# A scan fused with a gated feed-forward layer: decay rows loaded once, one chunk of them four times, and the opening reordered

## The chip, the cores and the metric

The kernel runs on one core of a Trainium2 chip. The metric is the device time of one execution in microseconds; a version's time is the median over its runs.

## What is computed

Two blocks follow each other. The first is a chunked state-space scan over 4 batches, 8 heads and 768 positions, with head width 32 and state width 16:

```python
log_a = np.log(np.clip(a, 1e-06, 1.0))
for c in range(nc):                       # chunks of 32 positions
    cum = np.cumsum(la, axis=-1)          # la, xc, Bc, Cc: this chunk
    L = np.exp(cum[:, :, :, None] - cum[:, :, None, :]) * causal
    M = np.einsum('bhin,bhjn->bhij', Cc, Bc) * L
    y_intra = np.einsum('bhij,bhjd->bhid', M, xc)
    y_inter = np.einsum('bhin,bhnd->bhid', Cc, state) * np.exp(cum)[:, :, :, None]
    y[:, :, sl] = y_intra + y_inter
    state = decay_full * state + np.sum(Bx, axis=2)
```

Its output, seen as 3072 tokens of 256 values, goes through the second block: `h = x @ w_in`, `g = h * sigmoid(1.702 h)`, `g @ w_out`, with 2048 hidden columns. The two weight matrices come in 64-bit floating point; the kernel turns them into 32-bit itself.

## The kernel before, in words

**Tiling.** The 768 positions are six groups (g) of 128, each of 4 batches, so 512 tokens. A group has two pairs (p) of batches; a pair's scan is worked out in sub-chunks of 64 positions (two SIDES). The hidden layer has 16 blocks (f) of 128 columns. Group 0 uses plain matmuls: `hidden(0, f)` for the 16 blocks, then `project_all(0)`. The later groups use a scheme with seven products of sums and differences. The order on each engine is the order of the program: `in_order` at the end of the kernel ties each instruction to the one before it on its engine, so an instruction that waits holds everything behind it on that engine.

**The weights.** They come in ten pieces (`PIECES`): pieces 0 to 3 hold two blocks of w_in each, 4 and 5 four blocks each, 6 to 9 four blocks of w_out each. `fetch(i)` issues two DMAs for a piece on SyncE's queue (SP), into one of four buffers; with `held=True` a small memset on VectorE (DVE) comes first, so that the DMA can't start ahead of that place in VectorE's order. A 64-bit number becomes a 32-bit one in steps: `fields(i)` on VectorE (step 0 takes the exponent bits, L188; step 1 the mantissa bits, L191), `clamp(i)` with two activations on ScalarE (ACT, L200 and L202), `rounded(i)` (L206) and `join(i)` (L220, L226) on VectorE. `narrow(i)` is `rounded(i)`, then `fields(i + 1)`, then `join(i)`: VectorE takes the next piece's fields before it joins the current piece, so a next piece that is not there yet holds the join too. `join` also fetches the pieces after the sixth (`NEXT`).

**The opening, group 0.** `az0` holds the first 128 positions of `a`, replicated four times over the partitions. From it come the sums of logarithms (`cum`); TensorE (PE) builds their differences (`differ`), ScalarE takes the exponentials (L529): one of 1024 columns for pair 0, four of 384 for pair 1. GpSimd (POOL) copies each pair's last decays into `drops` (`drop_of`, L452) and makes `CsT` (L583). VectorE turns blocks of C and B (`turn_blocks`, L541). Then `score` (L597) makes the scores of both pairs, `turn_back` (L555) transposes B back into positions, `weigh` (L608) multiplies the decays by the scores, in halves, `ends_first` (L458) multiplies the turned B by `drops`, `finish` (L724, L709) makes the outputs of the scan, `gain` (L628) the increment of the state, and `keep_first` (L644, ScalarE) copies it into the state S. In `finish`, `dense` (L416) issues products of ones into an unused part of a PSUM bank: they fill TensorE's time and no one reads them. `pads` does so with small ones at the very start.

**The decay rows of the later groups.** The tile `az` holds all 768 positions of `a` for 32 rows (batch, head), replicated four times: 128 partitions of 3 KB. One DMA loads it behind `fetch(5)`. `clip` limits it on VectorE and sets the first element of each sub-chunk to 0. `pick_a` (L372) takes chunk 1 of it on ScalarE, the only chunk taken so, for the decays of pair 2, which `fan_all` spreads on TensorE (L395). `store_a` writes the clipped rows to a scratch in device memory (32 partitions), from which `spread` (L259) reads the decays of the other pairs back, broadcast over partitions. `clip` stands in `store_a`, that is behind hidden block 5.

**Around the change** the work of the opening is written out by hand in the order in which the diff shows it. Behind it, `in_hidden[0]` lists what follows each hidden block: block 4 the loads of C and B for group 1 (GpSimd's queue, held by VectorE), block 5 `store_a`, block 6 `pick_a`, blocks 2 to 9 `narrow(1)` and on.

Of the kernel before, what the change touches and what calls it, by code (L numbers as in the profile page):

```python
# [8 lines left out]
FP32 = mybir.dt.float32  # L9
U32 = mybir.dt.uint32  # L10
BF16 = mybir.dt.bfloat16
AF = mybir.ActivationFunctionType
# [4 lines left out]
P = 128  # L17
# [18 lines left out]
def kernel(  # L36
# [66 lines left out]
    dram = ctx.enter_context(tc.tile_pool(name="dram", bufs=1, space=bass.MemoryType.DRAM))  # L103


    az = ffn.tile([P, 4 * TG // 2], FP32, tag="mg", name="az", bufs=3)[:, :NC * P].rearrange(
        "p (c s) -> p c s", c=NC)
    az0 = const.tile([P, P], FP32, name="az0")
    cum = const.tile([P, 2, P], FP32, name="cum")
    w_in = const.tile([P, NF, NK, P], FP32, name="w_in")  # L110
# [5 lines left out]
    def place(p):  # L116

        c, n = divmod(p, PG)
        return c, 2 * n
# [38 lines left out]
    def fetch(i, queue=nc.sync, held=False):  # L158
        name, f, n = PIECES[i]
        if n == 2 and f % 4:  # L160
            t = pieces.pop(i - 1)[:, 2 * n * DM:]
        else:
            t = pieces[i] = words(f"bits{i}")
            t = t[:, :2 * n * DM]
        if held:
            nc.vector.memset(t[:, :1], 0)
        if name == "in":
            src = moe_w_in[:, 2 * f * P:2 * (f + n) * P].rearrange("(k p) e -> p k e", p=P)
            dst, src = (v.rearrange(s, h=n, e=2 * P) for v, s in (
                (t, "p (h k e) -> k p h e"), (src, "p k (h e) -> k p h e")))  # L170
        else:
            src = moe_w_out[f * P:(f + n) * P, :].rearrange("(f p) (h e) -> h p f e", p=P, h=2)
            dst = t.rearrange("p (h f e) -> h p f e", h=2, f=n)
        for k in range(2):
            queue.dma_start(out=dst[k], in_=src[k])
        t = t.rearrange("p (e w) -> p e w", w=2)
        bits[i] = t[:, :, 0], t[:, :, 1]
# [156 lines left out]
    def fold_ident(k, engine=nc.vector):  # L334

        engine.tensor_tensor(
            out=idents[:, k * NH:(k + 1) * NH],
            in0=ident[:, :H].unsqueeze(1).to_broadcast([P, NH, H]),
            in1=ident[:, H:].unsqueeze(1).to_broadcast([P, NH, H]), op=ALU.add)
# [18 lines left out]

    def clip(t):

        nc.vector.tensor_scalar(out=t, in0=t, scalar1=1e-6, scalar2=1.0,
                                op0=ALU.max, op1=ALU.min)
        nc.vector.memset(t.rearrange(by_chunk, s=2)[:, :, :, 0], 0.0)

    def pick_a(p):

        c, b = place(p)
        X = ffn.tile([P, 2, DM], FP32, tag="ob", name=f"X{p}")
        X = fans[p] = X.rearrange("p k (q i) -> p k q i", q=Q)
        for k in range(2):  # L370
            for q in range(Q):
                nc.scalar.activation(X[:, k, q], az[:, c], AF.Copy, scale=pick[:, b + k, q:q + 1])  # L372


    Ls, BE, st = {}, {}, {}
# [32 lines left out]
    def pads(n, t):  # L408

        for i in range(n):  # L410
            c = 32 * (i % R)
            nc.tensor.matmul(out=t[c:c + 32, :32], lhsT=ones[:32, :32], rhs=ones[:32, :32],
                             start=True, stop=True, tile_position=(0, c), skip_group_check=True)

    def dense(t, n=4, start=True):
        nc.tensor.matmul(out=t[:, :n * H], lhsT=ones,  # L416
                         rhs=ones[:, :H].unsqueeze(1).to_broadcast([P, n, H]),
                         start=start, stop=True, skip_group_check=True)
# [167 lines left out]
    def score(pairs):  # L586

        cb = area(f"cb{pairs[0]}").rearrange("p r (k e) -> p r k e", k=2 * PG)
        for n, p in enumerate(pairs):
            s = st[p]  # L590
            BT, CT = s["BT"], s.pop("CT")
            s["cb"] = cb[:, :, 2 * n:2 * n + 2]
            for k in range(2):
                for i, side in enumerate(SIDES):
                    for r in range(R):
                        rows = slice(32 * r, 32 * r + 32)
                        nc.tensor.matmul(  # L597
                            out=s["cb"][side, r, k].rearrange("p (q i) -> p q i", q=Q),
                            lhsT=BT[rows, k, side], rhs=CT[rows, k, :, side],
                            start=True, stop=True, tile_position=(32 * r, H * i),  # L600
                            skip_group_check=True)

    def weigh(p, ks=(slice(0, 2),)):

        Lv = Ls[p].rearrange("p k r q i -> p k r (q i)")
        cb = st[p]["cb"].rearrange("p r k e -> p k r e")
        for k in ks:
            nc.vector.tensor_tensor(out=Lv[:, k], in0=Lv[:, k], in1=cb[:, k], op=ALU.mult)  # L608
# [66 lines left out]
    def finish(pairs, steps=range(2)):  # L675
# [58 lines left out]
        if early:  # L734
            def copied(i, t):
                nc.scalar.activation(
                    yT[g][:, t, cols].rearrange("p (k s i) -> p s k i", s=2, i=H)[:, i], y[i][t],
                    AF.Copy)

            if 0 in steps:  # L740
                dense(begun_y["banks"][0][:, 2 * P:])
                intra(0, pairs[0])
                return
            dense(begun_y["banks"][0][:, 2 * P:])
            intra(1, pairs[1])
            for t in range(NK):
                copied(0, t)
            for t in range(NK):
                for n, p in enumerate(pairs):
                    inter(n, p, (t,))  # L750
                copied(1, t)
        else:
            for step in steps:
                for n, p in enumerate(pairs):
                    (inter, intra)[step](n, p)
            if 1 not in steps:
                return
            for i in range(2):
                nc.scalar.activation(  # L759
                    yT[g][:, :, cols].rearrange("p t (k s i) -> p s t k i", s=2, i=H)[:, i], y[2][:, i],  # L760
                    AF.Copy)
# [287 lines left out]
        differ(p, [(r, ab[p, r]) for r in range(R)])  # L1049

    busy = bank("busy")
    pads(30, busy)
    both = area("ab0")
    for r in range(R):
        mask_banks(0, r, both[:, r])
# [19 lines left out]
    firsts[0] = ssd.tile([P, NB, P], FP32, tag="first", name="first", bufs=1)  # L1075
    nc.gpsimd.memset(firsts[0], 0.0)
    turn_blocks(0, "B")
    score(range(PG))
    turn_back()
    fold_ident(1)  # L1080
    weigh(0, (slice(0, 1),))
    fetch(1, held=True)
    weigh(0, (slice(1, 2),))
    for p in range(PG):
        ends_first(p)
    for i in range(2, 6):
        fetch(i, held=i == 2)
    nc.sync.dma_start(out=az.rearrange("p c s -> p (c s)"), in_=a.rearrange(
        "b h s -> (b h) s").unsqueeze(0).to_broadcast([R, NB * NH, NC * P]))
    fields(0, (0,))  # L1090
    for k in range(2):
        weigh(1, (slice(k, k + 1),))
    fields(0, (1,))
    rounded(0)
    finish(range(PG), (0,))
    gain(range(PG), (0,))
    clamp(0)
    keep_first(0)
    finish(range(PG), (1,))
    join(0, 2, (0,))  # L1100
# [12 lines left out]
    in_hidden = [{} for _ in range(NG)]  # L1113
    in_project = [{} for _ in range(NG)]
    def store_a():
        clip(az)
        for i, side in enumerate(SIDES):
            nc.sync.dma_start(out=scratch[:, i].rearrange("c r i -> r c i"), in_=az[:32, :, side])

    at(in_hidden[0], 4, lambda: gain(range(PG), (1,)), lambda: keep_first(1))  # L1120
    at(in_hidden[0], 5, store_a)
# [221 lines left out]
```

## Time and profile before

| what | value |
|---|---|
| runs shown | 353.86, 351.01, 354.13 us; median 353.86 |
| profiled execution | 352.01 us, of which the span is 350.3 us |
| TensorE busy | 341.9 us (98%) |
| VectorE / ScalarE / GpSimd busy | 255.8 / 149.5 / 40.7 us |
| bytes moved by DMA | 26.02 MB |
| granted TensorE clock | 1.0 |

All times are from the profiled execution and count from the start of its span. In the rows of a timeline stand start, duration, engine, line, operation, written tile and read tiles, shapes and count; a bracket holds the idle time of the engine just before and what ended it. A row with a count over one merges neighbours. "SPq" is the issue of a DMA on SyncE's queue, with the time that the issue took, not the transfer. "issue" is time in which the engine waited for nothing that the profile shows. In a row of windows stand, for each stretch, its length, each engine's busy time and count, the granted clock, the mean busy share of the DMA engines and the GB/s that they moved.

### The profile page before, as it was taken

To read this page: it belongs to the slowest core of one execution; us is meant where nothing else is said; L and a number is where in the kernel's file an instruction comes from. 1 tells how busy PE (TensorE), PEld (TensorE's weight loads), DVE (VectorE), ACT (ScalarE), POOL (GpSimd) and SP (SyncE) were. 2 spreads that over 40 slices of the span, in tenths; PEclk is the share of its full clock that TensorE was granted. 3 is DMA by queue.
4 is the path that set the end of the run, shared out by engine and by line. 5 is a ranking of instruction groups with operands and counts; after the bars stand their busy time and mean duration, and the time that the engine had idled before them with its cause. 6 is when DMAs were issued, how large, how long until landed. Compare 5 with 4: busy or idle time off the path is not lost.

```text
span 350.3 us, 8534 instructions
## 1 busy us (share of the span) xinstructions
PE 341.9 (98%) x3514; PEld 281.1 (80%) x3514; DVE 255.8 (73%) x476; ACT 149.5 (43%) x333; POOL 40.7 (12%) x78
## 2 busy tenths in 40 slices
PE   8897999999999999999999999999999999999996
PEld 6666874545688888888888888888888888899996
DVE  7787999999789988749986557986454654455463
ACT  6767774005254322743442444433554321554320
POOL 8305500300297000000000000000000000000000
PEclk9999999999999999999999999999999999999999
DMA  5699986533529000466122326120000120000221
GB/s 136 187 296 253 279 180 148 87 72 59 94 57 189 2 0 5 74 129 100 23 35 60 52 78 120 21 33 9 0 4 2 17 33 12 1 2 0 33 31 60
DMA packets 82784, 26.02 MB, mean 74 GB/s; under 512 B 68841, under 2 KB 81001, under 8 KB 82745
## 3 DMA queue, kind: packets, MB, share of 16 engines
q1 hardware_dynamic: 79864, 23.41, 32.0%
q0 software_dynamic: 1888, 1.74, 2.2%
q8 instruction: 27, 0.44, 0.5%
q10 hardware_dynamic: 992, 0.33, 0.4%
q14 instruction: 13, 0.10, 0.1%
HBM read 22.22 MB, written 3.24 MB: 73 GB/s over the span
## 4 chain that ended last, share of the span: by engine, by line
PE 79%; DVE 8%; DMA 6%; POOL 3%; SPq 2%; issue 1%; ACT 1%; POOLq 0%; DVEq 0%
PE acc L944 28%; PE X L842 19%; PE Y L852 14%; PE acc L951 7%; DMA bits<-in_moe_w_out_dram 4%; PE y L724 3%; PE h L786 2%; PE y L709 2%; PE o L884 2%; DVE p L220 2%; SPq L269 1%; PE cb L597 1%; DMA a<-scratch 1%; DVE m L206 1%; DVE L L608 1%
## 5 line engine op out<-in xcount | busy, mean ns | idle before, releaser
L847 ACT ACTIVATE ac<-X 128x256 f32<-128x256 f32 x76 | 29.0, 382 | 80.0 <-PE X L842 79.6
L944 PE MATMUL acc<-mg,mw 128*128 128x256 f32 x192 | 54.5, 379 | 0.0
L971 DVE TENSOR_TENSOR gT<-Y,ac 128x512 f32<-128x512 f32 x38 | 26.2, 690 | 37.2 <-PE Y L852 33.9
L819 ACT ACTIVATE gT<-gT 128x512 f32<-128x512 f32 (+1 forms) x76 | 39.3, 519 | 31.7 <-DVE gT L971 31.1
L842 PE MATMUL X<-my,mi 128*128 128x256 f32 x152 | 45.1, 379 | 0.0
L971 DVE TENSOR_TENSOR gT<-Y,b 128x256 f32<-128x256 f32 x38 | 15.8, 418 | 34.0 <-PE Y L852 34.0
L944 PEld LDWEIGHTS acc<-mg,mw 128*128 128x128 f32 x192 | 36.5, 190 | 5.0
L786 PE MATMUL h<-yT,w_in 128*128 128x128 f32 (+2 forms) x182 | 36.3, 357 | 2.0 <-DVE w_in L226 1.8
L944 PE MATMUL acc<-gT,w_out 128*128 128x256 f32 x128 | 35.5, 379 | 0.0
L786 PEld LDWEIGHTS h<-yT,w_in 128*128 128x128 f32 x182 | 26.8, 191 | 10.3 <-issue 5.6
L842 PEld LDWEIGHTS X<-my,mi 128*128 128x128 f32 x152 | 28.0, 190 | 3.7
L884 PE MATMUL o<-gT,w_out 128*128 128x512 f32 x64 | 28.6, 597 | 0.0
L810 DVE TENSOR_TENSOR mg<-gT 128x512 f32<-128x512 f32 x40 | 27.2, 680 | 0.0
L944 PEld LDWEIGHTS acc<-gT,w_out 128*128 128x128 f32 x128 | 24.2, 190 | 3.4 <-ACT yT L759 0.2
L847 ACT ACTIVATE b<-X 128x256 f32<-128x256 f32 x38 | 14.6, 383 | 20.4 <-PE X L842 20.0
L842 PE MATMUL X<-yT,w_in 128*128 128x256 f32 x76 | 23.2, 389 | 0.0
L852 PE MATMUL Y<-yT,w_in 128*128 128x256 f32 x76 | 22.7, 381 | 0.0
L852 PE MATMUL Y<-my,mi 128*128 128x256 f32 x76 | 22.6, 379 | 0.0
L842 PE MATMUL X<-my,w_in 128*128 128x256 f32 x76 | 22.6, 381 | 0.0
L852 PE MATMUL Y<-yT,mi 128*128 128x256 f32 x76 | 22.5, 379 | 0.0
L884 PEld LDWEIGHTS o<-gT,w_out 128*128 128x128 f32 x64 | 11.8, 190 | 13.2 <-issue 12.7
L387 DVE TENSOR_TENSOR_SCAN L<-a,idents 128x1024 f32<-128x1024 f32 x9 | 20.5, 2274 | 0.0
(140 smaller groups left out, 569.3 us busy)
## 6 DMA issues: line engine op xcount, KB each, us to landing
a<-scratch SPq DMA_DIRECT2D x18, 256.0 KB
bits<-in_moe_w_out_dram SPq DMA_DIRECT2D x8, 512.0 KB
x<-in_x_dram SPq DMA_DIRECT2D x20, 128.0 KB
bits<-in_moe_w_in_dram SPq DMA_DIRECT2D x8, 256.0 KB
bits<-in_moe_w_in_dram SPq DMA_DIRECT2D x4, 512.0 KB
out_dram<-ob SPq DMA_DIRECT2D x128, 16.0 KB
af<-in_a_dram SPq DMA_DIRECT2D x20, 64.0 KB
zC<-in_C_dram SPq DMA_DIRECT2D x36, 32.0 KB
```

What stands on the lines that cost most here:

```text
L387: nc.vector.tensor_tensor_scan(out=L, data0=ra[p].rearrange("p k e -> p (k e)"), data1=idents.rearrange("p h i -> p (h i)"), initial=0.0, ...
L724: nc.tensor.matmul(out=y[i][t][D * q:D * q + D, 2 * n + k], lhsT=rx[p][side, k, h], rhs=L[side, k, h // Q, h % Q], start=begin(i, t, (q,)) ...
L786: nc.tensor.matmul(out=h[:, cols], lhsT=w_in[:, f, k], rhs=yT[g][:, k, cols], start=(k == 0 and e == 0), stop=(k == NK - 1), skip_group_ch ...
L810: nc.vector.tensor_tensor(out=t[:, 0:2], in0=B[:, :, 1], in1=B[:, 0], op=ALU.subtract)
L819: nc.scalar.activation(o, i, AF.Silu, scale=GELU_SCALE)
L842: nc.tensor.matmul(out=s["X"], lhsT=lhsT, rhs=rhs, start=i == "1", stop=i == "4", skip_group_check=True)
L847: nc.scalar.activation(copy, s["X"], AF.Copy)
L852: nc.tensor.matmul(out=o, lhsT=lhsT, rhs=rhs, start=s.pop("new", False), stop=i != "5", skip_group_check=True)
L884: nc.tensor.matmul(out=o[c], lhsT=w_out[:, c, f], rhs=gT[g, f // 2][:, f % 2], start=(f == 0), stop=(f == NF - 1), skip_group_check=True)
L944: nc.tensor.matmul(out=acc[g][0][i], lhsT=w, rhs=h, start=(j == 0 and (i, 0) in begins), stop=(j == NF // 2 - 1), skip_group_check=True)
L951: nc.tensor.matmul(out=o[k] if type(o) is list else o[:, cols], lhsT=h[:, cols], rhs=w, start=(j == 0 and (i, k) in begins), stop=(j == NF ...
L971: nc.vector.tensor_tensor(out=o, in0=v, in1=w, op=ALU.add)
```

## The change

`az` shrinks to its 32 rows and is loaded without replication. A new tile `az1` holds chunk 1 alone, replicated four times, and `pick_a` reads it. Both are loaded between piece 1 and piece 2 of the weights, ahead of four pieces that the old load followed. Both are clipped right there on GpSimd, and `store_a` no longer clips. In the opening, `turn_back` and `fold_ident(1)` come ahead of `score`; both steps of `fields(0)`, `clamp(0)` and the two `ends_first` come ahead of the first weighing, where the ends and the first field stood between the weighings, the second field behind them and the clamp behind the gain. The `dense` ahead of the second pair's products goes, and `pads` issues 31 instead of 30.

```diff
-    az = ffn.tile([P, 4 * TG // 2], FP32, tag="mg", name="az", bufs=3)[:, :NC * P].rearrange(
+    az = ffn.tile([P, 4 * TG // 2], FP32, tag="mg", name="az", bufs=3)[:NB * NH, :NC * P].rearrange(
         "p (c s) -> p c s", c=NC)
+    az1 = const.tile([P, 1, P], FP32, name="az1")
...
     def clip(t):
-        nc.vector.tensor_scalar(out=t, in0=t, scalar1=1e-6, scalar2=1.0,
+        nc.gpsimd.tensor_scalar(out=t, in0=t, scalar1=1e-6, scalar2=1.0,
                                 op0=ALU.max, op1=ALU.min)
-        nc.vector.memset(t.rearrange(by_chunk, s=2)[:, :, :, 0], 0.0)
+        nc.gpsimd.memset(t.rearrange(by_chunk, s=2)[:, :, :, 0], 0.0)
...
-                nc.scalar.activation(X[:, k, q], az[:, c], AF.Copy, scale=pick[:, b + k, q:q + 1])
+                nc.scalar.activation(X[:, k, q], az1[:, 0], AF.Copy, scale=pick[:, b + k, q:q + 1])
...
-            dense(begun_y["banks"][0][:, 2 * P:])
             intra(1, pairs[1])
...
-    pads(30, busy)
+    pads(31, busy)
...
     turn_blocks(0, "B")
-    score(range(PG))
     turn_back()
     fold_ident(1)
+    score(range(PG))
+    fields(0)
+    clamp(0)
+    for p in range(PG):
+        ends_first(p)
     weigh(0, (slice(0, 1),))
     fetch(1, held=True)
+    rows = a.rearrange("b h s -> (b h) s")
+    nc.sync.dma_start(out=az1[:, 0], in_=rows[:, P:2 * P].unsqueeze(0).to_broadcast([R, NB * NH, P]))
+    nc.sync.dma_start(out=az.rearrange("p c s -> p (c s)"), in_=rows)
+    for t in az1, az:
+        clip(t)
     weigh(0, (slice(1, 2),))
-    for p in range(PG):
-        ends_first(p)
     for i in range(2, 6):
         fetch(i, held=i == 2)
-    nc.sync.dma_start(out=az.rearrange("p c s -> p (c s)"), in_=a.rearrange(
-        "b h s -> (b h) s").unsqueeze(0).to_broadcast([R, NB * NH, NC * P]))
-    fields(0, (0,))
     for k in range(2):
         weigh(1, (slice(k, k + 1),))
-    fields(0, (1,))
     rounded(0)
     finish(range(PG), (0,))
     gain(range(PG), (0,))
-    clamp(0)
     keep_first(0)
...
     def store_a():
-        clip(az)
         for i, side in enumerate(SIDES):
-            nc.sync.dma_start(out=scratch[:, i].rearrange("c r i -> r c i"), in_=az[:32, :, side])
+            nc.sync.dma_start(out=scratch[:, i].rearrange("c r i -> r c i"), in_=az[:, :, side])
```

More of the change, by code (lines that the diff above doesn't have):

```diff
@@ L359, in clip @@
     def clip(t):
-        nc.vector.tensor_scalar(out=t, in0=t, scalar1=1e-6, scalar2=1.0,
+        nc.gpsimd.tensor_scalar(out=t, in0=t, scalar1=1e-6, scalar2=1.0,
                                 op0=ALU.max, op1=ALU.min)
-        nc.vector.memset(t.rearrange(by_chunk, s=2)[:, :, :, 0], 0.0)
+        nc.gpsimd.memset(t.rearrange(by_chunk, s=2)[:, :, :, 0], 0.0)
     def pick_a(p):
         c, b = place(p)
+        assert c == 1
         X = ffn.tile([P, 2, DM], FP32, tag="ob", name=f"X{p}")
```

## The prediction

> **What bounds the kernel now.** I read the page first, then the waits of TensorE over the first 120 us.
>
> ```profile
> span 350.3 us, 8534 instructions
> PE 341.9 (98%) x3514; PEld 281.1 (80%) x3514; DVE 255.8 (73%) x476; ACT 149.5 (43%) x333; POOL 40.7 (12%) x78
> ...
> PE h L786 <- DVE w_in L226: 1.8, 1, 1.8
> ...
> PE y L709 <- DVE L L608: 0.8, 1, 0.8
> PE cb L597 <- issue: 0.7, 1, 0.7
> ```
>
> TensorE is busy for 98% of the span. Once the first hidden products have begun, its only waits worth naming are 1.8 us for w_in and 0.8 us for a weighing; the 0.7 us lie ahead of that. So an edit of the first 20 us can move the end in three ways alone: by when the hidden products start, and by what becomes of these two waits. Rows picked from the timeline (start, duration, engine, line) show the start and each wait with what precedes it; the rows between them are left out here and in the later fences.
>
> ```profile
> 0.82 0.73 SPq L272 DMA_DIRECT2D az<-in_a_dram  x1
> 7.75 2.77 ACT L529 ACTIVATE L<-ab 128x1024 f32<-128x1024 f32 x5
> 8.82 0.95 PE L597 MATMUL cb<-CT,Bt 32*64 32x128 f32 x45
> 10.50 0.65 PE L597 MATMUL cb<-CT,Bt 32*64 32x128 f32 x19 [0.73 <-issue]
> 10.59 0.21 POOL L452 COPY drops<-L 128x16 f32<-128x16 f32 x1 [0.17 <-ACT L L529]
> 11.08 0.66 PE L555 MATMUL b<-ident,Bt 128*128 128x128 f32 x4
> 11.26 1.29 DVE L608 TENSOR_TENSOR L<-L,cb 128x512 f32<-128x512 f32 x2 [2.06 <-POOL CsT L583]
> 12.00 2.30 SPq L175 DMA_DIRECT2D bits<-in_moe_w_in_dram  x3
> 12.47 0.75 DVE L458 TENSOR_TENSOR Be<-b,drops 128x256 f32<-128x256 f32 x2
> 13.48 1.28 DVE L608 TENSOR_TENSOR L<-L,cb 128x512 f32<-128x512 f32 x2
> 14.36 0.72 ACT L202 ACTIVATE p<-p,edge 128x512 uint32<-128x512 f32 x1
> 14.44 0.70 PE L416 MATMUL y<-ones 128*128 128x256 f32 x2
> 14.99 0.61 ACT L644 ACTIVATE S<-y,part 128x128 f32<-128x128 f32 x2
> 15.07 1.26 PE L724 MATMUL y<-L,x 64*32 64x64 f32 x64
> 17.42 2.84 PE L786 MATMUL h<-yT,w_in 128*128 128x512 f32 x6 [0.19 <-ACT yT L736]
> 19.15 1.68 SPq L1088 DMA_DIRECT2D az<-in_a_dram  x1
> 25.54 0.69 DVE L188 TENSOR_SCALAR p<-bits 128x1024 uint32<-128x1024 uint32 x1 [0.80 <-DMA bits<-in_moe_w_in_dram]
> 31.31 0.69 DVE L188 TENSOR_SCALAR p<-bits 128x1024 uint32<-128x1024 uint32 x1 [2.00 <-DMA bits<-in_moe_w_in_dram]
> 34.08 3.69 PE L786 MATMUL h<-yT,w_in 128*128 128x256 f32 x16 [1.82 <-DVE w_in L226]
> 35.18 0.55 DVE L361 TENSOR_SCALAR az<-az 128x768 f32<-128x768 f32 x1
> 37.77 0.69 DVE L188 TENSOR_SCALAR p<-bits 128x1024 uint32<-128x1024 uint32 x1 [0.78 <-DMA bits<-in_moe_w_out_dram]
> 74.97 1.16 PE L709 MATMUL y<-CsT,S 32*64 32x64 f32 x64 [0.79 <-DVE L L608]
> ```
>
> In the start, VectorE has a hole of 2.06 us before the first weighing (L608). The row names GpSimd's CsT, but by the code the weighing needs the scores (their last rows end near 11.15) and `drops`, not CsT; I take the scores as its releaser. The 1.82 us wait has this chain: the last w_in piece (5) lands near 31.2, VectorE takes its fields at 31.31, only then joins piece 4, and TensorE starts block 8 at 34.08, which is 2.77 us behind the landing. TensorE itself was ready at 32.26. The 0.79 us wait ends VectorE's chain; of its waits after 37.77 none is as long as 0.1 us, so that chain begins at the landing of piece 6.
>
> **The change, part by part.** *Transposes ahead of the scores.* Four transposes take 0.66 us with their drain, 0.5 in line. They write the bank that the first of the four later exponentials (L529) frees.
>
> One wide and four narrower exponentials end at 10.52; the scores started with the end of the wide one (8.82), so each narrower takes (10.52 - 8.82) / 4 = 0.42 us and the first ends at 9.25. The transposes run from 9.3 to 9.8, and the scores need 0.95 + 0.65 = 1.60 us: they end at 11.4, not 11.15, if the 0.73 us issue stall passes meanwhile, and at 12.1 if it comes again. I take 11.4.
>
> *Ends and fields into the hole.* The two ends cost 0.75 us. The two fields (0.42 us rows, a step of 0.34 us in line) cost 0.70. Together 1.45 us, which the hole of 2.06 would hold, had their inputs been there. The ends need `drops`, ready at 10.80. The fields stand ahead of them in VectorE's order and need the first w_in piece:
>
> ```profile
> q1 hardware_dynamic: 15, 0.01, 3.3%
> ```
>
> This is the DMA view between 9.3 and 11.2 us: SyncE's queue, whose next issue after the first piece is the row of 12.00, still moves 15 packets there, so I put that landing near 11.0. What stands behind the waiting field on VectorE is everything: ends, weighings, the hold on piece 1. Then the first weighing starts at 11.0 + 0.70 + 0.75 = 12.45, 1.2 us late. Were the piece there by 9.2, the scores would decide: 11.4. The four weighings, now in one row, need 2.5 us and end at 15.0 (before 14.76) or at 13.9.
>
> On TensorE the first pair's products and the gain follow the first weighing. The gain, which ended where the fill of 14.44 began, ends at 15.7 with no fill behind it (0.63 us saved). The second half of the second pair waits for the copy into S, which was held by the clamp until 15.0 and now follows the gain: 15.8 to 16.4 instead of 14.99 to 15.60. All behind it moves by the same 0.8, so the hidden products start at 18.2 instead of 17.42. With an early piece, the gain ends at 14.65, S at 15.3, and they start at 17.1. So the start moves by -0.3 to +0.8; I take +0.8. The clamp, two rows of 0.72 us, moves into ScalarE's time before 13.6, where it has nothing to do, and costs nothing; the 31st pad costs 0.02.
>
> *The loads of a.* Piece 1 is held by the first weighing and goes out at 13.2 (12.00 before; 12.1 if the piece was early). Two issues follow it, ahead of piece 2: az1 has the form of the 0.73 us row at 0.82, az lies between that and the 1.68 us at 19.15.
>
> ```profile
> 12.00:14.00 2.00, 1.84 (x79) 1.15 (x82) 2.00 (x6) 0.44 (x2) 0.10 (x1) 1.00 0.45 130
> ...
> 24.00:26.00 2.00, 2.00 (x11) 1.69 (x9) 1.17 (x3) 1.64 (x3) 0.00 (x0) 1.00 1.09 352
> 26.00:28.00 2.00, 2.00 (x40) 1.55 (x39) 1.97 (x4) 1.70 (x2) 0.00 (x0) 1.00 1.13 271
> 28.00:30.00 2.00, 2.00 (x11) 1.77 (x10) 1.31 (x3) 2.00 (x5) 1.52 (x3) 1.00 1.11 239
> 30.00:32.00 2.00, 2.00 (x11) 1.65 (x9) 0.69 (x2) 0.09 (x1) 2.00 (x4) 1.00 1.11 233
> ```
>
> With 0.73 us for az too (32 rows, where 128 took 1.68), and 0.45 us for each half of piece 1, piece 2 goes out at 13.2 + 0.9 + 1.46 = 15.6 (13.27 before), or at 14.5 with an early piece: 1.2 to 2.3 us late, and the az bytes (96 + 64 = 160 KB at 352 GB/s) add 0.45. The last two columns of the window rows are the DMA share and GB/s: the engines are under half busy at 12 to 14 and full from 24 on, so little is caught up. Against this stands what leaves: in the stretch in which the old 384 KB az runs, the rate falls from 352 to 248 (mean of the last three). If az is the cause, the 5.3 us up to piece 5's landing shrink by 5.3 x (1 - 248/352) = 1.6 us; if not, by nothing. Piece 5 moves by 1.2 to 2.3, + 0.45, - 1.6: 0.0 to +1.1 with az as the cause, up to +2.7 without. If the engines' backlog swallows the late issue, it gains: 0.45 - 1.6 = -1.1. Between -1.1 and +1.1 I take +0.3, nearer to the late end, because the idle share at 12 to 14 says that the issue counts.
>
> The Trainium skill bears on this (DMA: Bandwidth & Descriptors, Rules for kernel authors): a DMA whose outermost dimension is a broadcast of four copies runs on at most four of the sixteen engines. That the rate falls while the fourfold az is under way agrees; it speaks against az1, which stays fourfold: 64 KB over four engines at a sixteenth of 352 GB/s each are, as an estimate, 0.7 us on these ahead of pieces 2 to 5.
>
> *Clip on GpSimd.* VectorE loses 0.60 us of clip and memset between 35.18 and 35.78. On GpSimd the clips stand behind the memset of `first` and wait for az near 17; the loads of C and B queued behind them go out at 28.48 as before, being held by VectorE. The nearest GpSimd rows bound 768 elements:
>
> ```profile
> 11.57 0.53 POOL L1076 MEMSET first<- 128x512 f32 x1
> 58.62 1.22 DVE L226 SCALAR_TENSOR_TENSOR w_out<-m,p 128x1024 f32<-128x1024 f32 x1
> 65.05 3.29 POOL L583 TENSOR_TENSOR CsT<-Ct,since 128x256 f32<-128x256 f32 x2 [24.77 <-DVE since L478]
> 67.79 1.63 DVE L226 SCALAR_TENSOR_TENSOR w_out<-m,p 128x1024 f32<-128x1024 f32 x1
> ```
>
> From 0.53/512 to 1.65/256 us per element: 0.8 to 4.9 us; one input, so 1.0 us. VectorE's join beside GpSimd's two-input work took 1.63 us instead of 1.22, a third longer, so 1.0 us of clip may cost VectorE 0.3 us (1.6 at most) near 18. VectorE's 0.80 us wait at 25.54 covers that. The Trainium skill (GPSIMD Engine Reference, Specifications) says GpSimd shares its SBUF interfaces with VectorE and contends with instructions of two SBUF inputs; these two rows agree, and no term of the sum changes by it.
>
> *Sum.* TensorE reaches block 8 at 32.26 + 0.8 = 33.1 and block 8 may start at 34.08 + 0.3 = 34.4: the later start is hidden in the wait, and TensorE is 0.3 us late. VectorE from piece 5's fields to piece 6's took 31.31 to 36.99 with the clip, then waited 0.78. Without the clip it is at piece 6's fields at 31.6 + 5.1 = 36.7, and piece 6 no longer trails az: 1.0 us earlier than 37.77. At the second wait TensorE arrives at 74.18 + 0.3 = 74.5, VectorE's chain at 74.97 - 1.0 = 74.0: the wait is gone, and TensorE goes on 0.5 us earlier than before. 352.01 us is the profiled execution's own time (span 350.3 plus 1.7 around it), so 351.5. The runs shown are 353.86, 351.01 and 354.13; with the profiled one their mean is 352.75, and 3 us of scatter without any change means that 1% (3.5 us) is about what can be told. I put the forecast against that mean: 352.75 - 0.5, or **352.2 us**.
>
> **The rivals.** *Both waits go (B).* az was the drag and the engines' backlog hides the late issue: piece 5 at 30.1, block 8 allowed at 33.0, TensorE there at 33.1 (or 32.0 with an early first piece): -1.0, and 0.79 from the second wait, -1.8 in all: 350.9. The fall of the rate exactly while az runs speaks for it, the half-empty DMA engines of 12 to 14 against.
>
> *Slower (C).* One mechanism: the fields wait for the first piece, hold VectorE, and with it pieces 1 to 5; az was not the drag. Piece 5 lands 2.7 us late, block 8 starts at 36.8. VectorE reaches piece 6's fields at 31.31 + 2.7 + 5.1 = 39.1, so its chain ends at 76.3, TensorE at 76.9: 76.9 - 74.97 = +1.9, or 354.7. It decides once piece 5 is over 0.8 us late, the slack of the second wait. The 15 packets in flight after 9.3 speak for it, the removed 384 KB against.
>
> *The change doesn't do what it says (D).* The ends and fields leave the gap between the weighings, but the first weighing moves back as much and the wait for w_in ends where it did: piece 5 and 6 unmoved, only the clip's 0.6 us saved on a chain with 0.79 us of wait: between 0 and -0.6, 352.4.
>
> **How the numbers follow.** Forecast 0.38, B 0.24, C 0.24, D 0.14. The range takes B at its best (no wait at all at block 8, TensorE there at 32.0: -2.1 - 0.8, so 349.9) less some scatter, and C with 0.8 more, the part of GpSimd's upper 1.6 us that the 0.80 us wait doesn't cover (355.5): 349.5 to 355.5; the forecast's own is 351.2 to 353.4. Against the median of 353.86, over 1% faster is below 350.3: B in 0.55 of its cases, 0.13 of the forecast and little of D, some 0.19. Over 1% slower is above 357.4: C in 0.4 of its cases if the late pieces also push those of w_out behind them, and little else, 0.11. The rest is 0.70.
>
> **What would show it.** Right: the hole before the first L608 holds the two fields and the two ends; the first of these fields waits on DMA until about 11, the first weighing starts near 12.5, the four weighings follow each other; hidden products start near 18.2; block 8 after 34 still waits, by some 1.3 us; no 0.79 us wait near 74; no rate near 240 GB/s between 26 and 32. Wrong: the field shows no wait (then B), piece 5's fields start after 32.5 (then C), or matmuls of the hidden products take twice as long for some us, which nothing above contains.

## The result, and the profile after

| | median | range | runs |
|---|---|---|---|
| before | 353.97 us | 351.01 to 355.33 | 8 |
| after | 350.08 us | 348.74 to 350.66 | 8 |

The ratio is 0.9896, with a 95% interval from 0.9871 to 0.9921: the change makes the kernel 1.0% faster, 3.9 us by the medians. (The ratio goes by all runs and is not the quotient of the two medians. Measured a second time, below, it was 0.9938.) The profiled execution of after took 350.15 us with a span of 348.4 us; that of before, on which the prediction rests, took 352.01, below seven of its eight runs. The two profiles differ by 1.9 us, the medians by twice that.

First the page of after, and TensorE's waits in its first 120 us:

```profile
span 348.4 us, 8535 instructions
PE 341.9 (98%) x3514; PEld 280.4 (80%) x3514; DVE 256.5 (74%) x474; ACT 149.6 (43%) x333; POOL 45.6 (13%) x82
...
PE busy L414 <- DVE ones L309: 1.2, 1, 1.2
PE b L557 <- ACT L L531: 0.6, 1, 0.6
PE y L726 <- DVE bits L167: 0.5, 2, 0.3
PE h L787 <- DVE zC L127: 0.4, 1, 0.4
```

TensorE is as busy as before (341.9 us). The waits of 1.8 us for w_in and 0.8 us for a weighing are gone; in the stretch of the weights only 0.4 us is left. Next the timeline of after:

```profile
9.13 0.43 DVE L189 TENSOR_SCALAR p<-bits 128x512 uint32<-128x512 uint32 x1
10.23 1.21 PE L599 MATMUL cb<-CT,Bt 32*64 32x128 f32 x64
10.65 0.81 DVE L460 TENSOR_TENSOR Be<-b,drops 128x256 f32<-128x256 f32 x2 [0.77 <-POOL drops L454]
11.54 1.30 DVE L610 TENSOR_TENSOR L<-L,cb 128x512 f32<-128x512 f32 x2
17.09 9.39 PE L787 MATMUL h<-yT,w_in 128*128 128x512 f32 x30 [0.19 <-ACT yT L738]
18.27 2.77 POOL L362 TENSOR_SCALAR az<-az 32x768 f32<-32x768 f32 x1
18.33 1.31 DVE L207 SCALAR_TENSOR_TENSOR m<-bits,m 128x512 f32<-128x512 uint32 x1
20.35 0.97 DVE L189 TENSOR_SCALAR p<-bits 128x512 uint32<-128x512 uint32 x1
22.36 0.68 DVE L207 SCALAR_TENSOR_TENSOR m<-bits,m 128x512 f32<-128x512 uint32 x1
26.66 0.69 DVE L189 TENSOR_SCALAR p<-bits 128x1024 uint32<-128x1024 uint32 x1 [0.88 <-DMA bits<-in_moe_w_in_dram]
29.43 7.40 PE L787 MATMUL h<-yT,w_in 128*128 128x256 f32 x32 [0.44 <-DVE zC L127]
30.34 0.71 DVE L189 TENSOR_SCALAR p<-bits 128x1024 uint32<-128x1024 uint32 x1
35.37 0.71 DVE L189 TENSOR_SCALAR p<-bits 128x1024 uint32<-128x1024 uint32 x1
```

Here the field of piece 0 (9.13) waits for nothing, the hidden products start at 17.09 (17.42 before), pieces 5 and 6 (30.34, 35.37) are there when VectorE comes, and block 6 waits 0.44 us. (The row names VectorE's memset of zC, which ends at 29.28 right behind the join of block 6's weights, L227 at 28.59; by the code the block needs that join.) The transfer rates of after, by stretches of 2 us (last column, GB/s):

```profile
24.00:26.00 2.00, 2.00 (x10) 1.51 (x9) 1.74 (x4) 1.23 (x2) 0.00 (x0) 1.00 1.08 366
26.00:28.00 2.00, 2.00 (x40) 1.47 (x39) 1.34 (x3) 1.32 (x3) 0.00 (x0) 1.00 1.10 356
28.00:30.00 2.00, 1.56 (x8) 1.08 (x7) 1.97 (x4) 1.97 (x3) 0.40 (x1) 1.00 1.08 342
30.00:32.00 2.00, 2.00 (x11) 1.77 (x10) 2.00 (x4) 2.00 (x5) 2.00 (x3) 1.00 1.07 346
```

The rates of 239 and 233 between 28 and 32 have become 342 and 346.

### The profile page after: what moved, and what is told of

Read it like the earlier page. It is cut to its first block, busy times and chain, and to the rows that moved or that the text cites. A ratio compares the mean times of both kernels' runs of the same rounds, so it can differ in the third digit from the quotient of the medians.

```text
span 348.4 us, 8535 instructions
## 1 busy us (share of the span) xinstructions
PE 341.9 (98%) x3514; PEld 280.4 (80%) x3514; DVE 256.5 (74%) x474; ACT 149.6 (43%) x333; POOL 45.6 (13%) x82
## 4 chain that ended last, share of the span: by engine, by line
PE 91%; POOL 2%; DMA 2%; DVE 2%; SPq 1%; issue 1%; POOLq 0%; DVEq 0%
PE acc L945 28%; PE X L843 19%; PE Y L853 14%; PE o L885 8%; PE h L787 7%; PE acc L952 7%; DMA bits<-in_moe_w_in_dram 2%; PE y L726 2%; PE cb L599 2%; PE y L711 2%; PE A L630 1%; POOL x L146 1%; SPq L176 1%; POOL zB L130 1%; DVE L L610 0%
## 5 line engine op out<-in xcount | busy, mean ns | idle before, releaser
L787 PE MATMUL h<-yT,w_in 128*128 128x128 f32 (+2 forms) x182 | 37.0, 359 | 0.7 <-DVE zC L127 0.4
L1004 POOL DMA_DIRECT2D out_dram<-ob x32 | 17.4, 551 | 26.7 <-DVE ob L999 26.1
```

Source lines behind the costliest of these rows:

```text
L787: nc.tensor.matmul(out=h[:, cols], lhsT=w_in[:, f, k], rhs=yT[g][:, k, cols], start=(k == 0 and e == 0), stop=(k == NK - 1), skip_group_ch ...
L1004: (nc.sync if g else nc.gpsimd).dma_start(out=rows[:, b, :, cols], in_=t[32 * r:32 * r + 32, b * P:(b + 1) * P].rearrange("p (u e) -> p u ...
```

## The experiments

There are two questions: which part of the change brings the 3.9 us, and what holds back the rest. In each batch the kernels ran on one chip beside the kernel before; all ratios are against that.

| kernel | median, us (range, runs) | ratio, 95% interval |
|---|---|---|
| *first batch: before 353.89, 17 runs* | | |
| opening only | 353.54 (352.31 to 354.73, 12) | 0.9999 [0.9984, 1.0015] |
| rows only | 350.02 (349.59 to 350.32, 4) | 0.9894 [0.9875, 0.9912] |
| az as four DMAs | 350.46 (349.24 to 351.76, 6) | 0.9904 [0.9881, 0.9927] |
| before again | 353.78 (one execution) | none |
| *second batch: before 353.34, 17 runs* | | |
| az as two DMAs | 356.03 (354.85 to 356.71, 4) | 1.0069 [1.0044, 1.0093] |
| az1 as four DMAs | 352.03 (351.13 to 355.68, 12) | 0.9981 [0.9953, 1.0009] |
| rows late | 350.28 (349.04 to 352.90, 6) | 0.9915 [0.9886, 0.9945] |
| clip on VectorE | 350.82 (349.67 to 352.78, 6) | 0.9929 [0.9903, 0.9956] |
| *third batch: before 353.49, 18 runs* | | |
| after again | 350.38 (349.60 to 352.95, 12) | 0.9938 [0.9912, 0.9964] |
| fields back | 350.17 (348.84 to 350.82, 6) | 0.9908 [0.9875, 0.9941] |
| fields back, rows late | 349.27 (348.46 to 349.94, 6) | 0.9884 [0.9852, 0.9915] |
| rows only, late | 349.50 (349.20 to 351.52, 7) | 0.9903 [0.9870, 0.9936] |

### The two halves by themselves

**Opening only**: before with the new order of the opening and nothing else.

```diff
+    fields(0)
+    clamp(0)
+    for p in range(PG):
+        ends_first(p)
     weigh(0, (slice(0, 1),))
     fetch(1, held=True)
     weigh(0, (slice(1, 2),))
...
```

`turn_back` ahead of `score`, the `dense` that goes and the 31 pads are in it as well.

> Before with the reordered opening alone (turn back ahead of the scores, fields, clamp and ends ahead of the weighings, no second fill, 31 pads); the load and clip of az stay as before. Theory R (the old fourfold az drags the weight pieces, and that is what the change removes): the hidden products start about 0.3 us earlier, and the wait at block 8 grows by as much, so 0 to -0.4 us in all, with the wait of about 1.8 us and the one near 74 us still there. Theory O (the opening is what counts): more than half of the measured -3.9 us, so -2 us or more.

Measured: 0.9999. **Rows only**: before with the new tiles, loads and clips of a.

```diff
     weigh(0, (slice(0, 1),))
     fetch(1, held=True)
+    nc.sync.dma_start(out=az1[:, 0], in_=rows[:, P:2 * P].unsqueeze(0).to_broadcast([R, NB * NH, P]))
+    nc.sync.dma_start(out=az.rearrange("p c s -> p (c s)"), in_=rows)
+    for t in az1, az:
+        clip(t)
```

> Before with the new loads of a alone (32 rows once, chunk 1 four times, both between piece 1 and piece 2, clipped on GpSimd); the opening stays as before. Theory R: the wait at block 8 and the one near 74 us go, -2 us or more, and the hidden products start at about 17.4 us. Theory O: 0 to -0.8 us. If the two only work together, each alone gives less than 1 us.

Measured: 0.9894, the whole of the change's 0.9896. So the loads and clips bring all of it, and the opening nothing that shows, alone or on top of them. The opening-only timeline shows why its half can't be seen at the end:

```profile
17.67 8.88 PE L785 MATMUL h<-yT,w_in 128*128 128x512 f32 x30 [0.19 <-ACT yT L736]
...
34.15 0.56 DVE L361 TENSOR_SCALAR az<-az 128x768 f32<-128x768 f32 x1 [1.28 <-DMA az<-in_a_dram]
38.75 0.69 DVE L188 TENSOR_SCALAR p<-bits 128x1024 uint32<-128x1024 uint32 x1 [2.78 <-DMA bits<-in_moe_w_out_dram]
42.59 7.38 PE L785 MATMUL h<-yT,w_in 128*128 128x128 f32 x64 [1.86 <-DVE w_in L226]
```

The hidden products start at 17.67, where before's start at 17.1 to 17.4, and behind them stand waits for the old load of a and for piece 6 that no opening touches.

### Four engines for az, or its bytes?

**az as four DMAs**: before, with the same 384 KB into the same tile at the same place, as four plain copies of 32 rows.

```diff
-    nc.sync.dma_start(out=az.rearrange("p c s -> p (c s)"), in_=a.rearrange(
-        "b h s -> (b h) s").unsqueeze(0).to_broadcast([R, NB * NH, NC * P]))
+    rows = a.rearrange("b h s -> (b h) s")
+    for r in range(R):
+        nc.sync.dma_start(out=az[32 * r:32 * r + 32].rearrange("p c s -> p (c s)"), in_=rows)
```

> Before, with the same 384 KB of az at the same place, but as four DMAs of 32 rows instead of one DMA with a broadcast of four outermost. Theory R in the form that four DMA engines carry all of the old az: the bytes are the same but spread over all engines, so the rate between 26 and 32 us stays near 350 GB/s, piece 6 lands earlier, and -1 us or more. If the bytes themselves are the drag: no change within 0.5 us, and the rate still falls to near 250.

**Before again**, to see a second execution of before:

> The kernel before, unchanged, for a second profile. If the 8 runs of before, 351.0 to 355.3 us, scatter by the wait at block 8, this profile shows that wait or the one near 74 us at another length than 1.8 and 0.8 us, and the span differs by the same amount; if not, both waits are the same to 0.3 us and the span differs elsewhere.

**az as two DMAs**, each replicating twice:

```diff
+    for r in range(0, R, 2):
+        nc.sync.dma_start(out=az[32 * r:32 * r + 64].rearrange("p c s -> p (c s)"),
+                          in_=rows.unsqueeze(0).to_broadcast([2, NB * NH, NC * P]))
```

> Before, with the same 384 KB of az as two DMAs whose outermost broadcast is two, so that by theory R two DMA engines carry all of it (192 KB each) where four did. Theory R: az and the weights queued behind it on these engines land several us later than before, the product with the decays of chunk 1 and blocks behind it wait, +3 us or more. If the bytes or the repeated reading count and not the number of engines: within 0.5 us of before.

The same bytes without the replicated outermost dimension bring 353.89 - 350.46 = 3.4 us of the 3.9 us that rows only brought; with a twofold one they cost 356.03 - 353.34 = 2.7 us. The timeline of two DMAs:

```profile
37.51 0.66 DVE L361 TENSOR_SCALAR az<-az 128x768 f32<-128x768 f32 x1 [4.73 <-DMA az<-in_a_dram]
40.77 0.69 DVE L188 TENSOR_SCALAR p<-bits 128x1024 uint32<-128x1024 uint32 x1 [1.34 <-DMA bits<-in_moe_w_out_dram]
```

VectorE waits 4.73 us for az itself, and 1.34 more for piece 6. With four DMAs neither wait is there:

```profile
30.64 0.69 DVE L188 TENSOR_SCALAR p<-bits 128x1024 uint32<-128x1024 uint32 x1 [0.39 <-DMA bits<-in_moe_w_in_dram]
34.55 0.55 DVE L361 TENSOR_SCALAR az<-az 128x768 f32<-128x768 f32 x1
36.28 0.69 DVE L188 TENSOR_SCALAR p<-bits 128x1024 uint32<-128x1024 uint32 x1
```

The 2.7 us hold a second cost: behind TensorE's wait of 4.18 us for this load, the trace has its granted clock at 0.50 from 38.9 to 45.7 us. The one run of four with a mean clock of 1.0 took 356.14 us, so the loss does not rest on the clock alone.

So the drag is the spreading over few engines, not the amount. The semaphore of a weight DMA is raised in sixteen parts, that of the old load in before by four engines alone, between 31.8 and 33.7 us. Of the first of piece 6's two DMAs, which is queued behind the load, twelve parts landed by 30.1 us and four from 33.7 to 37.3 in the second execution of before (eleven by 30.7 and five from 33.2 to 35.8 in the first). With the two twofold DMAs fourteen landed by 30.3 us and two at 38.2 and 38.9. With the four plain DMAs all sixteen were there by 33.9, though issued 2.5 us later than in that second execution.

One sign that the theory expected stayed out. With the four plain DMAs the rate was to stay near 350 GB/s, and it fell too:

```profile
26.00:28.00 2.00, 2.00 (x10) 1.52 (x8) 2.00 (x4) 1.97 (x4) 0.00 (x0) 1.00 1.08 243
28.00:30.00 2.00, 2.00 (x39) 1.74 (x39) 1.97 (x4) 1.97 (x3) 0.59 (x1) 1.00 1.10 236
```

The kernel before has 271 and 239 there. So the fall of the rate, on which the prediction leaned, doesn't tell four engines from sixteen; the landings behind the load do. Whether fewer bytes are worth something beside it (350.02 against 350.46) lies within the intervals. The Trainium skill has this as a rule (DMA: Bandwidth & Descriptors, Rules for kernel authors): a leading broadcast of c copies, c below 16, confines a transfer to at most c engines; the ratios of 1.0069, 1 and 0.9904 for a twofold, a fourfold and no leading broadcast agree.

The second execution of before shows where an ordinary run of it loses the time, first in the waits of TensorE, then in the timeline:

```profile
PE h L786 <- DVE w_in L226: 1.9, 1, 1.9
PE ab L395 <- ACT X L372: 1.5, 1, 1.5
...
PE y L709 <- DVE L L608: 1.1, 1, 1.1
...
17.09 8.88 PE L786 MATMUL h<-yT,w_in 128*128 128x512 f32 x30 [0.19 <-ACT yT L736]
34.86 0.56 DVE L361 TENSOR_SCALAR az<-az 128x768 f32<-128x768 f32 x1 [1.86 <-DMA az<-in_a_dram]
39.54 0.70 DVE L188 TENSOR_SCALAR p<-bits 128x1024 uint32<-128x1024 uint32 x1 [2.87 <-DMA bits<-in_moe_w_out_dram]
43.39 7.38 PE L786 MATMUL h<-yT,w_in 128*128 128x128 f32 x64 [1.94 <-DVE w_in L226]
```

Its 353.78 us is within 0.2 us of the median of before. Its w_in wait is at block 12 (43.39), behind piece 6, not at block 8 behind piece 5; and the clip waits 1.86 us for az, which holds `pick_a` and, through it, TensorE for 1.5 us. The sum is 4.5 us, where the execution that the prediction read had 2.6. Against the 0.44 us of after, at the same start of the hidden products (17.09 in both), that is a difference of 4.1 us; the spans differ by 352.1 - 348.4 = 3.7.

### The place of the loads, az1 and the clip

**az1 as four DMAs**: after, with `az1` loaded by four copies of 32 rows.

```diff
-    nc.sync.dma_start(out=az1[:, 0], in_=rows[:, P:2 * P].unsqueeze(0).to_broadcast([R, NB * NH, P]))
+    for r in range(R):
+        nc.sync.dma_start(out=az1[32 * r:32 * r + 32, 0], in_=rows[:, P:2 * P])
```

> After, with the load of az1 (64 KB, a broadcast of four outermost) as four DMAs of 32 rows, so that no DMA is left on four engines. If the fourfold az1 still delays the weight pieces: -0.3 us or more against after (350.1 us), and less of the wait at block 6 (0.4 us in the profile). If 16 KB on four engines are too little to matter, or three more issues on SyncE ahead of piece 2 cost as much: within 0.3 us of after.

Measured: 352.03, with all twelve runs above 351.1, and in another batch than after. Neither expectation came. Its profile had the slow opening that the next part treats (hidden products at 19.82), and the three more issues show: piece 2 goes out at 17.40, where it does at 16.18 in the equally late opening of after again. What the fourfold az1 itself costs is not settled; with 0.44 us of wait for a piece left on TensorE in after, there is little to gain.

**Rows late**: after, with the loads and clips behind piece 5, where the old load stood.

```diff
     weigh(0, (slice(1, 2),))
     for i in range(2, 6):
         fetch(i, held=i == 2)
+    rows = a.rearrange("b h s -> (b h) s")
+    nc.sync.dma_start(out=az1[:, 0], in_=rows[:, P:2 * P].unsqueeze(0).to_broadcast([R, NB * NH, P]))
+    nc.sync.dma_start(out=az.rearrange("p c s -> p (c s)"), in_=rows)
+    for t in az1, az:
+        clip(t)
```

> After, with the loads of az1 and az and their clips behind piece 5, where the old az was loaded. If the place between piece 1 and 2 costs what it puts ahead of the pieces: the 0.9 us wait of VectorE for piece 4 and the 0.4 us wait at block 6 shrink, -0.4 us against after. If the place is what brings the gain, az1 comes too late for the product with the decays of chunk 1 and this kernel loses 1 us or more against after.

Measured: 350.28. The 0.44 us wait at block 6 is gone in its profile (span 347.3), yet the median is that of after: the place is worth less than the runs scatter.

**Clip on VectorE**: after, with the clips back in `store_a` on VectorE.

> After, with both clips on VectorE at their old place behind block 5 instead of on GpSimd. The profile of after shows VectorE's L207 at 18.33 with 1.31 us instead of 0.68 and L189 at 20.35 with 0.97 instead of 0.42 beside GpSimd's clip of 2.77 us. If that contention reaches the end: faster than after by 0.3 us or more. If VectorE's 0.88 us wait for piece 4 covers it, as forecast: within 0.3 us of after, and about 0.9 us of VectorE's work comes back in front of piece 6's fields, where no wait is left to hide it but TensorE has slack.

Measured: 350.82, with hidden products at 18.72, again a slow opening. That is 0.7 us above after's 350.08 of another batch, against both expectations, but its runs scatter by 3.1 us, and most of the gain is there. So moving the clip to GpSimd is not what brings the gain, though rows only and after contain it. What the clip costs on GpSimd stands in the rows of after above: 2.77 us for 32 rows of 768, and beside it VectorE's L207 took 1.31 us and L189 0.97, where the same instructions take 0.68 (22.36) and 0.43 (9.13) in the same timeline.

### Why the opening brings nothing

The starts of the hidden products had come out between 17.0 and 19.8 us. The traces give the time at which the last of the sixteen parts of the first piece's second DMA lands (fifteen are there by 9.5 in all):

| kernel (one execution each) | last part | first weighing | hidden products |
|---|---|---|---|
| *field ahead of the weighing:* after | 8.83 | 11.54 | 17.09 |
| opening only | 9.06 | 12.16 | 17.67 |
| rows late | 10.29 | 11.93 | 17.45 |
| clip on VectorE | 10.79 | 13.22 | 18.72 |
| az1 as four DMAs | 11.38 | 13.32 | 19.82 |
| after again | 11.41 | 13.33 | 19.85 |
| *field behind:* before | 11.00 | 11.26 | 17.42 |
| before again | 10.85 | 11.15 | 17.09 |
| rows only | 10.43 | 11.00 | 16.99 |
| az as two DMAs | 8.89 | 11.32 | 17.26 |
| az as four DMAs | 11.39 | 11.58 | 19.24 |
| fields back | 10.80 | 12.05 | 17.61 |
| fields back, rows late | 10.70 | 11.36 | 16.88 |
| rows only, late | 10.87 | 11.26 | 17.48 |

Where the field stands ahead and the piece lands after 10.7, the weighing and with it the products follow the piece; in the first three rows the scores end 0.1 us ahead of the weighing (at 11.44, 12.05 and 11.82) and set it. In clip on VectorE the two steps of the field also took longer beside GpSimd's CsT and memset (0.69 and 1.13 us, 0.43 and 0.41 in after). Where the field stands behind, a piece at 10.4 to 11.0 leaves the products at 16.9 to 17.6; az as four DMAs started its weighing in time, and its late products follow a stall behind it, shown in the last section. After again and the last three rows are of the third batch, which puts this to the test, with the edits (the fields and the clamp in their old places, transposes and ends left ahead; then also the loads late; then before's own opening with the loads late):

```diff
-    fields(0)
-    clamp(0)
     for p in range(PG):
         ends_first(p)
...
+    fields(0, (0,))
     for k in range(2):
         weigh(1, (slice(k, k + 1),))
+    fields(0, (1,))
     rounded(0)
     finish(range(PG), (0,))
     gain(range(PG), (0,))
+    clamp(0)
```

After again:

> The changed kernel once more, as the yardstick for the three that follow. Both theories: ratio to the kernel before near 0.990. Theory A (the first field, now ahead of the first weighing on VectorE, waits for the last sixteenth of the first piece of w_in; this part landed at 8.8 to 9.1 us in some executions and at 10.3 to 11.4 in most, and the wait eats what the earlier ends and transposes bring): if the piece lands after 10, the field's row shows a wait on DMA, the first weighing starts after 11.9 and the hidden products after 17.4; if it lands before 9.2, there is no wait and they start near 17.1. Theory B (the loads decide the stage up to block 6, so an earlier start is only a longer wait for pieces): the time doesn't follow the start of the hidden products.

Fields back:

> The changed kernel with the fields and the clamp of the first piece back in their old places (the first field between the two weighings' pairs, the second behind them, the clamp behind the gain); transposes and ends stay ahead, the loads and clips of a stay as changed. Theory A: nothing waits ahead of the first weighing, which starts at 11.3 to 11.8, the hidden products at 16.8 to 17.3 whenever the piece lands, and the time is 0.3 to 1.0 us below the changed kernel's of this batch. Theory B: the same early start, but VectorE's wait for piece 4 and TensorE's for block 6 grow by what was saved, and the time is within 0.3 us of the changed kernel's.

Fields back, rows late:

> As the kernel with the fields put back, and the two loads of a with their clips moved behind piece 5. The pieces go out about 1.2 us earlier, so no wait for piece 4 and none at block 6. Theory A: 349.0 to 349.7 us, the lowest of the batch, below both kernels. Theory B: about 0.4 us (the wait at block 6) below the kernel with the fields put back, and the start of the hidden products shows in the time once the loads no longer decide.

Rows only, late:

> The kernel before, its opening untouched, with only the new tiles, loads and clips of a, the loads behind piece 5 as in the kernel before. Hidden products start at 17.0 to 17.4. Theory A: the same as the kernel with fields put back and loads late, within 0.4 us, as the transposes and ends alone are worth at most that. Theory B: as the loads-and-clips-only kernel before it, 350.0 us, less the 0.8 us wait at block 6 that this showed, so near 349.3.

After again came to 0.9938, a smaller gain than the 0.990 expected, with three long runs among its twelve. Its profile drew the late case:

```profile
11.51 0.91 DVE L189 TENSOR_SCALAR p<-bits 128x512 uint32<-128x512 uint32 x1 [2.23 <-DMA bits<-in_moe_w_in_dram]
13.33 1.28 DVE L610 TENSOR_TENSOR L<-L,cb 128x512 f32<-128x512 f32 x2
11.60 0.67 PE L599 MATMUL cb<-CT,Bt 32*64 32x128 f32 x25 [0.63 <-issue]
14.06 0.35 PE L726 MATMUL y<-L,x 64*32 64x64 f32 x16 [1.16 <-DVE bits L167]
...
19.85 10.36 PE L787 MATMUL h<-yT,w_in 128*128 128x512 f32 x30
...
16.00:17.00 1.00, 1.00 (x66) 1.00 (x62) 0.96 (x3) 0.04 (x1) 0.00 (x0) 0.53 0.89 298
20.00:21.00 1.00, 1.00 (x2) 0.48 (x3) 1.00 (x1) 0.97 (x3) 1.00 (x1) 0.50 1.09 351
23.00:24.00 1.00, 1.00 (x3) 0.38 (x2) 0.96 (x4) 0.97 (x2) 0.00 (x0) 1.00 1.03 346
```

The field waits 2.23 us, the weighing behind it starts at 13.33, TensorE is left without work and its granted clock (the column ahead of the DMA share) then stands at 0.50 from 16 to 23 us. This execution took 352.95 us, the longest of the twelve. Of the twelve, three lie at 352.7 to 353.0 with a mean clock of 0.989, and seven at 349.6 to 350.4 with a clock of 0.998 or more. With the fields back in their places no run is above 350.82, though the piece is late (10.80) in its profile too, and the mean of the runs falls from 351.0 to 350.1 us; the medians are 0.2 us apart, and the scatter of the two kernels covers both differences. Of all runs with a clock on record, five of the 56 with the field ahead have a mean clock of 0.99 or below, and none of over 80 with it behind, az as two DMAs left aside. In fields back the weighing started at 12.05, later than expected, as the scores ended later. The rest of that saving does become a wait for pieces, as theory B had it; the timeline of fields back:

```profile
27.22 0.69 DVE L189 TENSOR_SCALAR p<-bits 128x1024 uint32<-128x1024 uint32 x1 [1.84 <-DMA bits<-in_moe_w_in_dram]
30.02 7.37 PE L787 MATMUL h<-yT,w_in 128*128 128x256 f32 x32 [1.03 <-DVE zC L127]
```

Piece 4 comes 1.84 us late for VectorE, and block 6 waits 1.03 (0.88 and 0.44 in after). With both, the fields back and the loads late, this is gone:

```profile
11.36 1.30 DVE L610 TENSOR_TENSOR L<-L,cb 128x512 f32<-128x512 f32 x2
16.88 8.88 PE L787 MATMUL h<-yT,w_in 128*128 128x512 f32 x30 [0.19 <-ACT yT L738]
24.12 0.69 DVE L189 TENSOR_SCALAR p<-bits 128x1024 uint32<-128x1024 uint32 x1
26.27 8.90 PE L787 MATMUL h<-yT,w_in 128*128 128x256 f32 x40
```

No wait for a piece, none at block 6, hidden products at 16.88: 349.27 us, the lowest of the batch, 1.1 us below after's 350.38 beside it, with all six runs below after's median. It is faster than both kernels, than after by 1.7 us in the means. Rows only, late comes to 349.50, so the earlier transposes and ends are worth 0.2 us by the medians, within the scatter. Both theories hold a part: the wait of the field is seen in the one long run of after that has a trace, with whose clock the two other long ones agree, and the loads decide the usual runs.

## Why the prediction was right or wrong

The direction was right, and so was the old load of a as the drag. Where this drag falls was wrong, and with it the size: 0.5 us was forecast and 3.9 measured. By its steps:

- **Transposes ahead of the scores** (11.4 for their end): 10.23 + 1.21 = 11.44 in after, without the issue stall; 12.27 in after again, with it, where 12.1 had been named.
- **Ends and fields into the hole** (field at 11.0, weighing at 12.45, hidden products at 18.2, or 17.1 with an early piece). After's profile shows the early piece, at its bound: weighing at 11.54, products at 17.09. After again shows the late one, worse than forecast: 13.33 and 19.85. Both cases were named with their cause. What was not seen is that the one kernel falls into either from run to run, and that TensorE, left idle, can fall to half its clock, as it did there.
- **The loads of a.** This is the step that failed: the term of 1.6 us off the landing of piece 5. The prediction read the wait at block 8 as the old load's drag on piece 5. But piece 5 goes out ahead of that load (17.51 against 19.15 in before), and there only a single part of it was late: fifteen of the sixteen of its second DMA had landed by 28.4, the last at 31.18. In the three other profiles with the old load or its twofold form (before again, opening only, az as two DMAs) piece 5 is whole at 28.1 to 28.8, and no one waits for it. That wait belonged to the one execution; what held its last part is open, and that rival B had it go is in part luck. What the old load holds is itself and the pieces behind it: in before again TensorE waits 1.5 us for az, 1.9 behind piece 6, and 1.1 at the end of VectorE's chain, 4.5 us that all go. The prediction put the wait for az at nothing, as its execution shows none at the clip (35.18). It shows none because the late piece 5 held VectorE some 2.2 us longer (31.31 against 29.06 in before again); without that, VectorE would have been there ahead of az, which landed at 33.7. Piece 6 was given 1.0 us, and that counted at the second wait alone. Then the -0.5 was set against the mean of 352.75, below the median of 353.97 of the eight runs.
- **The late issue.** Piece 2 went out 1.5 us later (14.75 against 13.27), inside the 1.2 to 2.3. Piece 5 landed at 29.6, that is 0.8 us later than in before again, and earlier than in the execution that the prediction read; it was forecast 0.3 later than there. What was left of it for TensorE is 0.44 us at block 6.
- **The clip on GpSimd.** 2.77 us for the 768 elements, 3.5 with az1's 0.75, instead of 1.0, inside the bound of 4.9; and VectorE lost (1.31 - 0.68) + (0.97 - 0.43) = 1.2 us instead of 0.3, inside the bound of 1.6. VectorE's wait for piece 4 covered it, as forecast. The row that it was priced by, GpSimd's memset, was too cheap a neighbour: 1.0 ns an element, where the clip took 3.6 and the two-input row 6.4.
- **The second wait** (0.79 us at 74): gone, as forecast.
- **The rivals.** B is what after's profile shows: both waits gone, and the late issue swallowed but for the 0.44 us. Its -1.8 is near the 1.9 us between the two spans; between ordinary runs the difference is 3.9, and its mechanism, the drag on piece 5, is not in them. Of C's conditions the waiting field exists, but az was the drag, so the price did not follow. D was wrong: against the execution that it read, pieces 5 and 6 came earlier and the wait for w_in at block 8 went.

## What to carry to other kernels

A transfer that only four of sixteen engines carry delays whatever is queued behind it on these four, not what went out ahead of it. Split it into plain copies before cutting its bytes. Before sizing a wait from a profile, see where the profiled execution stands among the runs: one below the median has some of the waits too small, and the missing part may be just what an edit removes. A second profile of the same kernel tells which waits are its own and which belong to one execution. Work that fills a hole must not stand in an in-order queue behind data that may come late, if what follows it in the queue would have been ready.

## What the runs showed of the hardware

The last of the sixteen parts of the first weight piece landed at 10.3 to 11.4 us in eleven of the fourteen profiled executions and by 9.1 us, with the others, in three; the same program (after, and after again) gave both. A half clock followed gaps on TensorE in three executions: 6.8 us of it in after again, whose longest gaps from 9 us on are 1.16 and 0.63 us, 3.4 us in az1 as four DMAs (gap of 1.66), 6.8 us in az as two DMAs (wait of 4.18). Clip on VectorE, with a gap of 2.00 us, and az as four DMAs, with 1.65, kept their clock. In these traces the clock changes at whole multiples of 3.41 us from its first record. In the stretch of that length ahead of the fall TensorE was busy for 58%, 44% and 2%; clip on VectorE kept its clock after 65%, but before again did so after 57%, so what decides stays open. So does the late start of az as four DMAs (hidden products at 19.24), behind a stall of 1.65 us for which the trace names no releaser. One timeline row of each:

```profile
13.94 0.35 PE L726 MATMUL y<-L,x 64*32 64x64 f32 x16 [2.00 <-DVE bits L167]
...
17.27 0.87 PE L724 MATMUL y<-L,x 64*32 64x64 f32 x63 [1.65 <-issue]
```

Beside the clip on GpSimd VectorE lost time in one or two instructions and was not slower throughout. In after, L207 took 1.31 us and L189 0.97, where they take 0.68 and 0.43 without it, but the two rows between them (L221 and L227, at 19.56 and 20.01) took their usual 0.41 and 0.42. In fields back, L221 took 0.88 beside the clip and L189 its usual 0.42. The Trainium skill (GPSIMD Engine Reference, Specifications) says that GpSimd shares its SBUF interfaces with VectorE and names VectorE instructions in a 2-port perf mode or with two SBUF inputs for the contention; L207 and L221 have two, L189 has one, and no row shows in which mode it ran.
